# A decode attention block: V products as full-width matmuls, the copy of the products moved behind the next exp, wq loaded first

## The chip, the cores and the metric

The kernel runs on one core of a Trainium2 chip. The metric is the device time of one execution in microseconds: the median of the runs is given for the kernel before. The views of the profile come from one profiled execution on the chip. Its engines are called PE (the matrix engine; PEld is its weight load), DVE (VectorE), ACT (ScalarE), POOL and SP (which issues the loads).

## The reference

One step of decoding for 8 sequences (B = 8, one token each, D = 512). The input is normalised, goes through attention over a cached window and, beside that, through a gated feed-forward network (FFN); the result is x + s * g.

```
xn = layernorm(x)
q  = xn @ wq                        # 32 heads of 128
k, v = the last 1024 positions of the caches, 8 kv heads, each used by 4 q heads
p  = softmax(q @ k.T / sqrt(128))   # per batch and head, over 1024 positions
s  = (p @ v) @ wo
g  = silu((gelu(xn @ w_gate) * (xn @ w_up)) @ w_down)     # F = 1792
out = x + s * g
```

All tensors are bf16. For every batch 2 MB of K and 2 MB of V are read; with the weights that makes 47.46 MB from HBM.

## The kernel before

**Loads.** All large loads go to one ring of eight slots of 16 KB per partition (2 MB each). `load_k` and `load_v` fill a slot with the K or V of one batch in two loads of 1 MB, one for each half of the kv heads (g = 0, 1). SP issues them in the order of the program. Each load waits for its slot to be free and for one of eight semaphores, so the load eight places earlier must have landed. The order is: K 0, wq (two loads of 2 MB), K 1, V 0, and then in iteration b of the loop K b+2 and V b+1. After the loop come gate, up, down and the pieces of wo. The small x goes on ACT's queue.

**Start.** The constants are built on DVE and POOL (L101 to L224: the identity, the mask `neg_st`, `neg_mv`, the selectors `sel`, `own`, `pick`, and a cleared `oT`). The layernorm of x gives `xnR`. DVE turns both halves of K 0 (`turn_k`, L235), and clears `qbd` (L240). The q products (L248) are 32 matmuls of 512 columns into eight PSUM banks; ACT and DVE cast them (L258), DVE turns them (L261), and 16 small copies (L270) place them in `qbd`, a block-diagonal stationary operand.

**Loop over the batches.** Everything is issued in the order of the program on each engine. In iteration b:
- `turn_k(b+1, 0)` turns the first half of the next K on DVE;
- `softmax(b)`: the maximum `mx` on DVE (L306) and its reduction over the four partition groups (L311, L313), `nb` and the exp with its sums on ACT (L316, L318);
- `scores(b+1, 0)`: two mask matmuls (L285) and eight score matmuls of 512 columns (L296) on PE;
- `gather(b-1)`: PE adds the four partition groups of the previous batch's products with `sel` (L361) and the sums (L365), in fp32, into `o_ps`, which holds four batches;
- `turn_k(b+1, 1)` and `scores(b+1, 1)`, the second half;
- `turn_p(b)` turns the probabilities on DVE (L329);
- `values(b)`: the V products (L340), 64 matmuls with 32 stationary and 128 moving columns, which go to four column groups of PE in turn;
- `keep_o(b)`: ACT copies the products from `O_ps` to SBUF (L353). `O_ps` has two buffers.

After batch 4, `regroup(0)` works on the first four batches: the reciprocal of the sums (L376) and a product (L378) on DVE, eight matmuls to `r_ps` on PE (L389), and a cast to `oT` on DVE (L392). On PE these stand behind the V products of batch 4, and on DVE the cast stands ahead of `turn_k(6, 0)`.

**Tail.** `gather(7)`, `regroup(1)`, then the FFN: `z_ps` and `u_ps` (L451), the gelu on ACT and DVE (L461 to L471), a turn (L474), `f_ps` (L480), the gate `g_sb`; then `s_ps`, 128 small matmuls over wo in the order in which its pieces land (L499), `y` (L507), `out_sb` (L509) and the store.

Of the kernel before, what the change touches and what calls it, by code (L numbers as in the profile page):

```python
# [8 lines left out]
ALU = mybir.AluOpType  # L9
AX = mybir.AxisListType  # L10
BF16 = mybir.dt.bfloat16
FP32 = mybir.dt.float32
I32 = mybir.dt.int32
PSUM = bass.MemoryType.PSUM
# [7 lines left out]
def kernel(  # L22
# [13 lines left out]
    nc = tc.nc  # L36

    B, Sq, D = A_x.shape
    Hkv, Sk, Dh = A_k_cache.shape[1], A_k_cache.shape[2], A_k_cache.shape[3]
    Hq = A_wq.shape[1] // Dh  # L40
# [5 lines left out]
    P = nc.NUM_PARTITIONS  # L46
    NK = D // P
    HG = 4
    NG = Hkv // HG
    C = W * HG // P  # L50
# [6 lines left out]
    consts = ctx.enter_context(tc.tile_pool(name="consts", bufs=1))  # L57
    keep = ctx.enter_context(tc.tile_pool(name="keep", bufs=1))
    two = ctx.enter_context(tc.tile_pool(name="two", bufs=2))
    ring = ctx.enter_context(tc.tile_pool(name="ring", bufs=N_SLOTS))  # L60

    def slot(name):
        return ring.tile([P, 2 * ROW], BF16, name=name, tag="slot")
# [6 lines left out]
    def load_cache(cache, b, name):  # L70
        t = slot(name).rearrange("p (g x) -> p g x", g=NG)
        for g in range(NG):
            nc.sync.dma_start(  # L73
                out=t[:, g],
                in_=cache[b, g * HG : (g + 1) * HG, win0:Sk, :].rearrange(
                    "n (p c) d -> p n (c d)", c=C
                ),
            )
        return t

    k_sb, v_sb = {}, {}

    def load_k(b):
        k_sb[b] = load_cache(A_k_cache, b, "k_sb")

    def load_v(b):
        v_sb[b] = load_cache(A_v_cache, b, "v_sb")

    load_k(0)
    wq_v = A_wq.rearrange("(p k) n -> p k n", k=NK)  # L90
    wq_sb = []
    for i in range(2):
        t = slot("wq_sb").rearrange("p (k n) -> p k n", k=NK // 2)
        nc.sync.dma_start(out=t, in_=wq_v[:, i * (NK // 2) : (i + 1) * (NK // 2), :])  # L94
        wq_sb += [t[:, k, :] for k in range(NK // 2)]
    load_k(1)
    load_v(0)


    ident = consts.tile([P, P], BF16, name="ident")  # L100
    nc.vector.memset(ident, 0.0)  # L101
    nc.gpsimd.affine_select(
        out=ident,
        in_=ident,
# [13 lines left out]
        out=xpad,  # L118
        in_=xpad,
# [17 lines left out]
        out=xhat,  # L137
# [9 lines left out]
    with tc.tile_pool(name="ps_x", bufs=1, space=PSUM) as ps_x:  # L147
# [7 lines left out]
        for t in range(4):  # L155
# [4 lines left out]
                start=True,  # L160
                stop=True,
# [5 lines left out]
    qd = Hq // NG  # L167
# [6 lines left out]
        out=hv,  # L174
        in_=hv,
# [7 lines left out]
        out=neg_st,  # L183
        in_=neg_st,
# [8 lines left out]
        out=neg_mv,  # L193
        in_=neg_mv,
# [7 lines left out]


    NU = Hq // 8
    sel = consts.tile([P, NG, Hq], FP32, name="sel")
    nc.vector.memset(sel, 0.0)
    for g in range(NG):
        nc.vector.tensor_reduce(
            out=sel[:, g, g * qd : (g + 1) * qd],
            in_=ident.rearrange("p (t g h) -> p g h t", t=4, g=NG)[:, g],  # L210
            axis=AX.X,
            op=ALU.add,
        )
    own = consts.tile([P, 8], FP32, name="own")
    nc.vector.tensor_reduce(
        out=own, in_=ident.rearrange("p (i e) -> p e i", e=8), axis=AX.X, op=ALU.add
    )
    pick = consts.tile([P, 4 * NU], BF16, name="pick")
    with nc.allow_low_precision(reason="sums of zeros and a single one"):
        nc.vector.tensor_reduce(  # L220
            out=pick, in_=ident.rearrange("p (a e) -> p a e", e=8), axis=AX.X, op=ALU.add
# [7 lines left out]
    qbd = keep.tile([P, 2, B, 2, NG, 4 * Hq], BF16, name="qbd")  # L229
# [3 lines left out]
    def turn_k(b, g):  # L233
        t = kT_pool.tile([P, ROW], BF16, name="kT")
        nc.vector.transpose(out=t.bitcast(I32), in_=k_sb[b][:, g].bitcast(I32))  # L235
        kT[b, g] = t

    turn_k(0, 0)
    turn_k(0, 1)
    nc.vector.memset(qbd, 0.0)  # L240
    q_both = slot("q_both")
    q_bf = q_both[:, 0:ROW]
    q_t = q_both[:, ROW : 2 * ROW]
    with tc.tile_pool(name="ps_q", bufs=1, space=PSUM) as ps_q:
        q_ps = [ps_q.tile([P, 512], FP32, name=f"q_ps{i}") for i in range(8)]
        for k in range(NK):
            for i in range(8):
# [4 lines left out]
                    start=(k == 0),  # L252
                    stop=(k == NK - 1),
# [10 lines left out]
    for j in range(4):  # L264
        sl = slice(32 * j, 32 * j + 32)
        for m in range(2):
            for g in range(NG):
                e = nc.scalar.copy if (4 * j + 2 * m + g) % 3 == 2 else nc.vector.tensor_copy
                c0 = j * Hq + g * qd
                e(out=qbd[sl, m, :, :, g, c0 : c0 + qd], in_=q_v[sl, m, :, 0, :, g, :])  # L270


    pT, S, P_sb, O_ps = {}, {}, {}, {}
    sums = keep.tile([P, B], FP32, name="sums")

    actx = ExitStack()
    ps_s = actx.enter_context(tc.tile_pool(name="ps_s", bufs=2, space=PSUM))
    ps_o = actx.enter_context(tc.tile_pool(name="ps_o", bufs=2, space=PSUM))
    ps_g = actx.enter_context(tc.tile_pool(name="ps_g", bufs=1, space=PSUM))

    def scores(b, g):
# [22 lines left out]
    def softmax(b):  # L304
        mx = two.tile([P, 1], FP32, name="mx")
        nc.vector.tensor_reduce(  # L306
            out=mx, in_=S[b].rearrange("p a c -> p (a c)"), axis=AX.X, op=ALU.max
        )

        m2 = two.tile([64, 1], FP32, name="m2")  # L310
        nc.vector.tensor_tensor(out=m2, in0=mx[0:64, :], in1=mx[64:128, :], op=ALU.max)  # L311
        m1 = two.tile([32, 1], FP32, name="m1")
        nc.vector.tensor_tensor(out=m1, in0=m2[0:32, :], in1=m2[32:64, :], op=ALU.max)  # L313
        nb = two.tile([P, 1], FP32, name="nb")
        for j in range(4):
            nc.scalar.mul(nb[32 * j : 32 * j + 32, :], m1, -inv)  # L316
        P_sb[b] = two.tile([P, C // 2, 32, 2], BF16, name="P_sb")
        nc.scalar.activation(  # L318
            out=P_sb[b].rearrange("p c i w -> p c w i"),
            in_=S[b].rearrange("p a (c w i) -> p (a c) w i", w=2, i=32),  # L320
            func=ACT.Exp,
            bias=nb,
            scale=inv,
            accum_out=sums[:, b : b + 1],
        )

    def turn_p(b):
        pT[b] = two.tile([P, C // 2, Hq, 2], BF16, name="pT")
        nc.vector.transpose(  # L329
            out=pT[b].rearrange("p c h w -> p (c h w)").bitcast(I32),  # L330
            in_=P_sb[b].rearrange("p c i w -> p (c i w)").bitcast(I32),
        )

    def values(b):
        O_ps[b] = ps_o.tile([P, NG, Dh], FP32, name="O_ps")
        for g in range(NG):
            vv = v_sb[b][:, g].rearrange("p (c d) -> p c d", d=Dh)
            for c in range(C):
                t = c % 4
                nc.tensor.matmul(  # L340
                    O_ps[b][32 * t : 32 * t + 32, g, :],
                    pT[b][:, c // 2, :, c % 2],
                    vv[:, c, :],
                    start=(c < 4),
                    stop=(c >= C - 4),
                )

    o_ps = {}
    O_sb = {}

    def keep_o(b):
        O_sb[b] = two.tile([P, NG, Dh], FP32, name="O_sb")
        nc.scalar.copy(out=O_sb[b], in_=O_ps[b])  # L353

    def gather(b):
        q = b % 4
        if q == 0:
            o_ps[b // 4] = ps_g.tile([P, Dh + 1], FP32, name="o_ps")
        o = o_ps[b // 4][32 * q : 32 * q + 32, :]
        for g in range(NG):  # L360
            nc.tensor.matmul(  # L361
                o[:, 0:Dh], sel[:, g, :], O_sb[b][:, g, :], start=(g == 0), stop=(g == NG - 1)
            )
        for g in range(NG):
            nc.tensor.matmul(  # L365
                o[:, Dh : Dh + 1],
                sel[:, g, :],
                sums[:, b : b + 1],
                start=(g == 0),
                stop=(g == NG - 1),  # L370
            )

    def regroup(q):

# [24 lines left out]
    for b in range(B):  # L399
        if b + 2 < B:  # L400
            load_k(b + 2)
        if b + 1 < B:
            load_v(b + 1)
            turn_k(b + 1, 0)
        softmax(b)
        if b + 1 < B:
            scores(b + 1, 0)
        if b >= 1:
            gather(b - 1)
        if b + 1 < B:  # L410
            turn_k(b + 1, 1)
            scores(b + 1, 1)
        turn_p(b)
        values(b)
        keep_o(b)
        if b == 4:
            regroup(0)

# [9 lines left out]
    for u in range(NU):  # L428
        if u % 2 == 0:
            pair = slot("wo_sb").rearrange("p (v j d) -> p v j d", v=2, d=D)  # L430
        t = pair[:, u % 2]
# [5 lines left out]
            nc.sync.dma_start(out=t[:, a:z, :], in_=src[:, a:z, :])  # L437
        wo.append(t)

    gather(B - 1)  # L440
    regroup(1)
    actx.close()
# [4 lines left out]
    for n, ws in (("z_ps", wgu[0]), ("u_ps", wgu[1])):  # L447
        ps = ps_f.tile([P, FT], FP32, name=n)
        for k in range(NK):
            for t in range(4):  # L450
# [4 lines left out]
                    start=(k == 0),  # L455
                    stop=(k == NK - 1),
# [6 lines left out]
        out=z2, in0=z2, scalar1=0.044715, scalar2=1.0, op0=ALU.mult, op1=ALU.add  # L463
# [11 lines left out]
        out=hT.rearrange("p j b -> p (j b)"), in_=h_bf.rearrange("p (y j) -> p j y", j=NJ)  # L475
    )
    f_ps = ps_f.tile([P, DT], FP32, name="f_ps")
    for j in range(NJ):
        for t in range(4):
# [4 lines left out]
                start=(j == 0),  # L484
                stop=(j == NJ - 1),
# [4 lines left out]
        out=g_sb, in0=g_sb, scalar1=0.5, scalar2=0.5, op0=ALU.mult, op1=ALU.add  # L490
# [5 lines left out]
    for u in range(NU):  # L496
        for j in range(8):
            for t in range(4):
# [4 lines left out]
                    start=(u == 0 and j == 0),  # L503
                    stop=(u == NU - 1 and j == 7),
# [7 lines left out]
        out=out_f.rearrange("b (t d) -> t b d", t=4), in_=out_sb[0 : P : RB, :]  # L512
# [31 lines left out]
```

## Time and profile before

| | |
|---|---|
| median of 3 runs | 121.66 us (121.61 to 121.68) |
| the profiled execution | 121.48 us, its span 119.4 us |
| PE busy | 73.0 us (61%), 985 matmul records |
| DVE busy | 75.8 us (63%) |
| ACT busy | 31.4 us (26%) |
| HBM read | 47.46 MB, 397 GB/s over the span |
| main load queue | 94.3% of 16 engines' span |

The span runs from the first to the last instruction of the execution; the execution's own time has 2.1 us around it. The page cuts the span into 40 slices of about 3 us; a digit is the busy share of a slice in tenths, and the row PEclk is the granted clock of PE in tenths of full speed. A line of the timeline gives the start and the duration in us, the engine, the line of the kernel, the operation, the tiles (out<-in), how many instructions are merged, and in brackets the idle time before them and what ended it. Matmul durations include the way through the array, so the distance between starts is what one costs in a row.

### The profile page before, as it was taken

Reading aid. Unit: us, or ns where it says so; the run is one execution under the profiler, and the core shown is the slowest. Engines: PE = TensorE matmul, PEld = TensorE weight load, DVE = VectorE, ACT = ScalarE, POOL = GpSimd, SP = SyncE. Lnnn points to the kernel's source line nnn. Section 1 sums busy time; section 2 is a strip of 40 time slices with the busy share of each in tenths; the row PEclk is TensorE's granted clock in tenths of the full one; section 3 lists DMA queues with packets and bytes.
Section 4 is the critical chain, followed back from the end, with each engine's and each line's share of the span. In section 5 each row is a group of like instructions: output and inputs, shape, how many; then the busy total and the mean of one; then the engine's idle time right before and its main releaser. Section 6 shows DMA issues by size and latency. Waiting matters only on the chain.

```text
span 119.4 us, 2300 instructions
## 1 busy us (share of the span) xinstructions
PE 73.0 (61%) x985; PEld 38.7 (32%) x992; DVE 75.8 (63%) x101; ACT 31.4 (26%) x75; POOL 3.2 (3%) x10
## 2 busy tenths in 40 slices
PE   0001499811994987969687674991994547545370
PEld 0000134300341544535443351450453433143350
DVE  1048978399739999999959959909943241651000
ACT  2233000676007052341712510700616211200000
POOL 2006100000000000000000000000000000000000
PEclk9999999985599999999999998599589855555555
DMA  1999999999999999999999999999999999999930
GB/s 47 411 445 417 434 425 431 417 428 434 428 420 425 431 423 423 428 423 431 417 431 420 431 423 423 428 428 423 420 434 439 437 433 418 427 421 417 412 148 3
DMA packets 6254, 47.61 MB, mean 399 GB/s; under 512 B 732, under 2 KB 868, under 8 KB 1124
## 3 DMA queue, kind: packets, MB, share of 16 engines
q1 hardware_dynamic: 6228, 47.46, 94.3%
q8 instruction: 8, 0.13, 0.4%
q10 hardware_dynamic: 16, 0.01, 0.0%
q14 instruction: 2, 0.02, 0.0%
HBM read 47.46 MB, written 0.01 MB: 397 GB/s over the span
## 4 chain that ended last, share of the span: by engine, by line
DMA 85%; DVE 6%; PE 4%; SPq 2%; issue 1%
DMA k_sb<-in_A_k_cache_dram 48%; DMA wo_sb<-in_A_wo_dram 20%; DMA v_sb<-in_A_v_cache_dram 17%; DVE kT L235 4%; PE S_ps L296 2%; PE s_ps L499 1%; SPq L73 1%; DVE mx L306 1%; SPq L94 1%; PE O_ps L340 1%; PE r_ps L389 1%; DVE y L507 0%; DVE out_sb L509 0%; DVE oT L392 0%; DVE m L311 0%
## 5 line engine op out<-in xcount | busy, mean ns | idle before, releaser
L296 PE MATMUL S_ps<-kT,qbd 128*128 128x512 bf16 x128 | 34.1, 413 | 15.5 <-DVE kT L235 11.9
L235 DVE STREAM_TRANSPOSE kT<-k_sb 128x2048 int32<-128x2048 int32 x16 | 36.5, 2289 | 4.4 <-DMA k_sb<-in_A_k_cache_dram 4.3
L296 PEld LDWEIGHTS <-qbd 128*128 128x128 bf16 x128 | 12.8, 102 | 31.9 <-issue 16.4
L248 PE MATMUL q_ps<-wq_sb,xnR 128*128 128x512 bf16 x32 | 9.8, 481 | 4.3 <-DMA wq_sb<-in_A_wq_dram 4.3
L316 ACT ACTIVATE nb<-m 32x1 f32<-32x1 f32 x32 | 6.4, 201 | 22.5 <-DVE m L313 22.2
L306 DVE TENSOR_REDUCE mx<-S_ps 128x1 f32<-128x1024 f32 x8 | 9.6, 1196 | 4.1 <-PE S_ps L296 4.1
L318 ACT ACTIVATE P_sb<-S_ps,nb 128x1024 bf16<-128x1024 f32 x8 | 11.1, 1390 | 0.3
L340 PE MATMUL O_ps<-v_sb,pT 128*32 128x128 bf16 x512 | 9.1, 226 | 2.6 <-DVE pT L329 2.6
L340 PEld LDWEIGHTS <-pT 128*32 128x32 bf16 x512 | 7.6, 100 | 5.6 <-issue 3.0
L353 ACT COPY O_sb<-O_ps 128x256 f32<-128x256 f32 x8 | 3.0, 372 | 23.3 <-PE O_ps L340 23.3
L329 DVE STREAM_TRANSPOSE pT<-P_sb 128x512 int32<-128x512 int32 x8 | 5.7, 711 | 3.4 <-ACT P_sb L318 3.3
L248 PEld LDWEIGHTS <-xnR 128*128 128x128 bf16 x32 | 3.7, 118 | 10.1 <-issue 8.1
L361 PE MATMUL o_ps<-O_sb,sel 128*32 128x128 f32 x32 | 6.3, 332 | 0.9 <-ACT O_sb L353 0.9
L499 PE MATMUL s_ps<-wo_sb,oT 128*32 128x128 bf16 x128 | 4.4, 307 | 3.7 <-DMA wo_sb<-in_A_wo_dram 3.7
L258 ACT CAST q_both<-q_ps 128x512 bf16<-128x512 f32 x6 | 3.0, 611 | 12.2 <-PE q_ps L248 12.2
L151 PE MATMUL xnT_ps<-ident,xhat 8*128 8x8 bf16 x4 | 0.3, 174 | 8.9 <-DVE xhat L136 8.9
L499 PEld LDWEIGHTS <-oT 128*32 128x32 bf16 x128 | 3.5, 136 | 4.7 <-issue 4.5
L361 PEld LDWEIGHTS o_ps<-O_sb,sel 128*32 128x32 f32 x32 | 3.4, 128 | 5.0 <-issue 1.7
L507 DVE TENSOR_TENSOR y<-s_ps,g_sb 128x128 f32<-128x128 f32 x1 | 0.3, 292 | 7.2 <-PE s_ps L499 7.2
L285 PE MATMUL S_ps<-neg_mv,neg_st 128*128 128x512 bf16 x9 | 3.3, 384 | 1.9 <-DVE q_both L258 1.9
L129 DVE BATCH_NORM_STATS2 stats<-x_sb 8x6 f32<-8x512 bf16 x1 | 0.7, 681 | 5.7 <-DMA x_sb<-in_A_x_dram 5.7
L240 DVE MEMSET qbd<- 128x4096 uint32 x1 | 3.5, 3472 | 0.8 <-issue 0.8
(64 smaller groups left out, 51.2 us busy)
## 6 DMA issues: line engine op xcount, KB each, us to landing
k_sb<-in_A_k_cache_dram SPq DMA_DIRECT2D x16, 1024.0 KB, 19.7
v_sb<-in_A_v_cache_dram SPq DMA_DIRECT2D x16, 1024.0 KB, 20.0
wq_sb<-in_A_wq_dram SPq DMA_DIRECT2D x2, 2048.0 KB, 11.4
wo_sb<-in_A_wo_dram SPq DMA_DIRECT2D x3, 1024.0 KB, 25.1
wgu_sb<-in_B_w_gate_dram SPq DMA_DIRECT2D x1, 1792.0 KB, 21.4
wgu_sb<-in_B_w_up_dram SPq DMA_DIRECT2D x1, 1792.0 KB
wd_sb<-in_B_w_down_dram SPq DMA_DIRECT2D x1, 1792.0 KB
wo_sb<-in_A_wo_dram SPq DMA_DIRECT2D x1, 640.0 KB
```

Source lines behind the costliest of these rows:

```text
L235: nc.vector.transpose(out=t.bitcast(I32), in_=k_sb[b][:, g].bitcast(I32))
L240: nc.vector.memset(qbd, 0.0)
L248: nc.tensor.matmul(q_ps[i], xnR[:, k, :, :].rearrange("p j b -> p (j b)"), wq_sb[k][:, i * 512 : (i + 1) * 512], start=(k == 0), stop=(k = ...
L285: nc.tensor.matmul(S[b][:, half, :], neg_st.rearrange("p j h -> p (j h)"), neg_mv.rearrange("p a n -> p (a n)"), start=True, stop=False,)
L296: nc.tensor.matmul(S[b][:, half, :], qbd[:, m, b, w, g, :], kv[:, half * 16 : (half + 1) * 16, m, :, w], start=False, stop=(g == NG - 1 an ...
L306: nc.vector.tensor_reduce(out=mx, in_=S[b].rearrange("p a c -> p (a c)"), axis=AX.X, op=ALU.max)
L316: nc.scalar.mul(nb[32 * j : 32 * j + 32, :], m1, -inv)
L318: nc.scalar.activation(out=P_sb[b].rearrange("p c i w -> p c w i"), in_=S[b].rearrange("p a (c w i) -> p (a c) w i", w=2, i=32), func=ACT.Exp,
L329: nc.vector.transpose(out=pT[b].rearrange("p c h w -> p (c h w)").bitcast(I32), in_=P_sb[b].rearrange("p c i w -> p (c i w)").bitcast(I32),)
L340: nc.tensor.matmul(O_ps[b][32 * t : 32 * t + 32, g, :], pT[b][:, c // 2, :, c % 2], vv[:, c, :], start=(c < 4), stop=(c >= C - 4),)
L361: nc.tensor.matmul(o[:, 0:Dh], sel[:, g, :], O_sb[b][:, g, :], start=(g == 0), stop=(g == NG - 1))
L499: nc.tensor.matmul(s_ps[32 * t : 32 * t + 32, :], oT[:, j, u, :], wo[u][:, j, t * DT : (t + 1) * DT], start=(u == 0 and j == 0), stop=(u = ...
```

## The change

- **V products.** `values` now takes four of the 32 chunks of positions at a time: a stationary operand of 128 columns (four chunks x 32 heads) and 512 moving columns (four chunks x 128), 16 matmuls per batch instead of 64. Of the 4 x 4 blocks of each result only the four on the diagonal are wanted. `O_ps` is four times as wide, two PSUM banks, and has one buffer instead of two.
- **Copy and gather.** `keep_o` copies the upper and the lower 64 partitions with the two blocks that each needs; `sel` has one more dimension to pick the diagonal; the gather has four products instead of two, and one product for the sums instead of two, with a selector `sel_s` of its own.
- **Order on ACT.** The copy of batch b-1's products is issued after the exp of batch b, not at the end of iteration b-1.
- **Start.** wq is loaded ahead of K of batch 0; on DVE `qbd` is cleared before K 0 is turned, and the second half of K 0 is turned after the copies to `qbd`.
- **Addresses.** An unused tile `pad` of 128 bytes per partition is allocated; with it the ring starts on a multiple of 512 bytes, as it did.

```diff
-    load_k(0)
     wq_v = A_wq.rearrange("(p k) n -> p k n", k=NK)
...
+    load_k(0)
     load_k(1)
     load_v(0)
...
-    sel = consts.tile([P, NG, Hq], FP32, name="sel")
+    sel = consts.tile([P, NG, 2, Hq], FP32, name="sel")
...
+    consts.tile([P, 32], FP32, name="pad")
+    sel_s = consts.tile([P, Hq], FP32, name="sel_s")
...
+    nc.vector.memset(qbd, 0.0)
     turn_k(0, 0)
-    turn_k(0, 1)
-    nc.vector.memset(qbd, 0.0)
...
+    turn_k(0, 1)
...
-    ps_o = actx.enter_context(tc.tile_pool(name="ps_o", bufs=2, space=PSUM))
+    ps_o = actx.enter_context(tc.tile_pool(name="ps_o", bufs=1, space=PSUM))
...
-        O_ps[b] = ps_o.tile([P, NG, Dh], FP32, name="O_ps")
+        O_ps[b] = ps_o.tile([P, NG, 4 * Dh], FP32, name="O_ps")
         for g in range(NG):
-            vv = v_sb[b][:, g].rearrange("p (c d) -> p c d", d=Dh)
-            for c in range(C):
-                t = c % 4
+            vv = v_sb[b][:, g]
+            for c in range(0, C, 4):
                 nc.tensor.matmul(
-                    O_ps[b][32 * t : 32 * t + 32, g, :],
-                    pT[b][:, c // 2, :, c % 2],
-                    vv[:, c, :],
-                    start=(c < 4),
-                    stop=(c >= C - 4),
+                    O_ps[b][:, g, :],
+                    pT[b][:, c // 2 : c // 2 + 2].rearrange("p c h w -> p (c h w)"),
+                    vv[:, c * Dh : (c + 4) * Dh],
+                    start=(c == 0),
+                    stop=(c == C - 4),
                 )
...
-        O_sb[b] = two.tile([P, NG, Dh], FP32, name="O_sb")
-        nc.scalar.copy(out=O_sb[b], in_=O_ps[b])
+        O_sb[b] = two.tile([P, NG, 2, Dh], FP32, name="O_sb")
+        for a in range(2):
+            rows = slice(64 * a, 64 * a + 64)
+            nc.scalar.copy(
+                out=O_sb[b][rows].rearrange("p g w d -> p g (w d)"),
+                in_=O_ps[b][rows, :, 2 * a * Dh : 2 * (a + 1) * Dh],
+            )
...
-            nc.tensor.matmul(
-                o[:, 0:Dh], sel[:, g, :], O_sb[b][:, g, :], start=(g == 0), stop=(g == NG - 1)
-            )
-        for g in range(NG):
-            nc.tensor.matmul(
-                o[:, Dh : Dh + 1],
-                sel[:, g, :],
-                sums[:, b : b + 1],
-                start=(g == 0),
-                stop=(g == NG - 1),
-            )
+            for w in range(2):
+                nc.tensor.matmul(
+                    o[:, 0:Dh],
+                    sel[:, g, w, :],
+                    O_sb[b][:, g, w, :],
+                    start=(g == 0 and w == 0),
+                    stop=(g == NG - 1 and w == 1),
+                )
+        nc.tensor.matmul(
+            o[:, Dh : Dh + 1], sel_s, sums[:, b : b + 1], start=True, stop=True
+        )
...
         softmax(b)
+        if b >= 1:
+            keep_o(b - 1)
...
         values(b)
-        keep_o(b)
...
+    keep_o(B - 1)
     gather(B - 1)
```

More of the change, by code (lines that the diff above doesn't have):

```diff
@@ L208 @@
         nc.vector.tensor_reduce(
-            out=sel[:, g, g * qd : (g + 1) * qd],
-            in_=ident.rearrange("p (t g h) -> p g h t", t=4, g=NG)[:, g],
+            out=sel[:, g, :, g * qd : (g + 1) * qd],
+            in_=ident.rearrange("p (a g h w) -> p g w h a", a=2, g=NG, w=2)[:, g],
             axis=AX.X,
@@ L213 @@
         )
+    consts.tile([P, 32], FP32, name="pad")
+    sel_s = consts.tile([P, Hq], FP32, name="sel_s")
+    nc.vector.tensor_reduce(
+        out=sel_s, in_=ident.rearrange("p (j h) -> p h j", j=4), axis=AX.X, op=ALU.add
+    )
     own = consts.tile([P, 8], FP32, name="own")
@@ L360, in gather @@
         for g in range(NG):
-            nc.tensor.matmul(
-                o[:, 0:Dh], sel[:, g, :], O_sb[b][:, g, :], start=(g == 0), stop=(g == NG - 1)
-            )
-        for g in range(NG):
-            nc.tensor.matmul(
-                o[:, Dh : Dh + 1],
-                sel[:, g, :],
-                sums[:, b : b + 1],
-                start=(g == 0),
-                stop=(g == NG - 1),
-            )
+            for w in range(2):
[8 more added lines that the diff above has]
+            o[:, Dh : Dh + 1], sel_s, sums[:, b : b + 1], start=True, stop=True
+        )
     def regroup(q):
```

## The prediction

> **What bounds the kernel now.** I read the slices of the page first, then its chain, then the timeline of one middle batch, of the place where batch 4 ends, and of the tail. M(b) below is the start of `mx` (L306) in batch b.
>
> The slices: clock, DMA and rate.
>
> ```profile
> PEclk9999999985599999999999998599589855555555
> DMA  1999999999999999999999999999999999999930
> GB/s 47 411 445 417 434 425 431 417 428 434 428 420 425 431 423 423 428 423 431 417 431 420 431 423 423 428 428 423 420 434 439 437 433 418 427 421 417 412 148 3
> ```
>
> The DMA row is full from slice 2 on: 47.46 MB go through at about 425 GB/s without a hole, and the last weights land at 114.8. The chain agrees:
>
> ```profile
> DMA 85%; DVE 6%; PE 4%; SPq 2%; issue 1%
> ```
>
> So compute counts only where it makes the end wait, or makes the queue run dry. Slot waits do not make it dry: a cache load takes about 20 us from issue to landing (section 6 of the page), so some 8 MB are queued ahead. The question is how late compute may be. One batch of the timeline, columns start, us, engine, line:
>
> ```profile
> 48.34 1.19 DVE L306 TENSOR_REDUCE mx<-S_ps 128x1 f32<-128x1024 f32 x1
> 50.52 0.62 PE L361 MATMUL o_ps<-O_sb,sel 128*32 128x128 f32 x4
> 50.80 1.39 ACT L318 ACTIVATE P_sb<-S_ps,nb 128x1024 bf16<-128x1024 f32 x1
> 52.17 1.90 PE L296 MATMUL S_ps<-kT,qbd 128*128 128x512 bf16 x8 [0.93 <-DVE kT L235]
> 54.00 1.08 PE L340 MATMUL O_ps<-v_sb,pT 128*32 128x128 bf16 x64
> 55.10 1.19 DVE L306 TENSOR_REDUCE mx<-S_ps 128x1 f32<-128x1024 f32 x1
> ```
>
> The period is 6.76 us, and VectorE is full in it (1.19 + 0.3 + 2.29 + 0.71 + 2.27); PE has gaps. A batch of cache takes the queue 9.85 us (K of batch 5 lands at 61.08, of batch 6 at 70.9), so from batch 4 on M(b) is set by K: 63.3, 73.2, 83.05. The end of batch 4, and the tail:
>
> ```profile
> 69.99 0.66 PE L389 MATMUL r_ps<-pick,o_x 128*128 128x16 bf16 x8
> 70.68 0.43 DVE L392 CAST oT<-r_ps 128x128 bf16<-128x128 f32 x1 [1.35 <-PE r_ps L389]
> 70.92 2.32 DVE L235 STREAM_TRANSPOSE kT<-k_sb 128x2048 int32<-128x2048 int32 x1
> ...
> 89.18 1.23 DVE L306 TENSOR_REDUCE mx<-S_ps 128x1 f32<-128x1024 f32 x1 [1.49 <-PE S_ps L296]
> 98.70 0.67 PE L389 MATMUL r_ps<-pick,o_x 128*128 128x16 bf16 x8 [1.58 <-DVE o_x L378]
> 106.28 1.69 PE L480 MATMUL f_ps<-wd_sb,hT 128*32 128x128 bf16 x56 [2.90 <-DVE hT L474]
> 108.38 1.04 PE L499 MATMUL s_ps<-wo_sb,oT 128*32 128x128 bf16 x32 [0.41 <-DMA wo_sb<-in_A_wo_dram]
> 114.84 1.25 PE L499 MATMUL s_ps<-wo_sb,oT 128*32 128x128 bf16 x32 [0.49 <-DMA wo_sb<-in_A_wo_dram]
> 116.15 0.29 DVE L507 TENSOR_TENSOR y<-s_ps,g_sb 128x128 f32<-128x128 f32 x1 [7.20 <-PE s_ps L499]
> ```
>
> Two things are to be seen. VectorE, which works in order, cannot turn the next K (70.92) before the `oT` cast, and that waits for `r_ps`, which PE issues behind the V products of batch 4; today this ends just as K lands. And after `r_ps` of the tail the FFN runs and then waits for wo. Slack of the tail: f_ps and s_ps need 1.36 (106.28 to the next weight load at 107.64) + 4 x 0.87 (1.04 less the end of the last matmul) = 4.85 us of PE at the half clock seen there, so f_ps could start at 116.15 - 0.3 - 4.85 = 111.0, and `r_ps`, 7.6 earlier, at 103.4. **The slack is 4.7 us** over 98.70.
>
> **The change, part by part**, against the profiled execution: 121.48 us, span 119.4, 2.1 around it. The median of the runs is 0.18 above it.
>
> *V products.* Out: 64 matmuls, 1.08 us. In: 16 of 512 columns on a 128-column weight. The scores have that shape: 18 in a row took 3.81 us in the q products (from 19.21: 0.212 each); at a granted clock of 0.50 the scores of batch 0 started every 0.43 us (29.36, 29.78, 30.21). So 3.4 us, or 6.8 cold, per batch: +2.3, or more. [...]
>
> *Gather.* From L361 to L365 four fp32 passes took 0.46 (43.76 to 44.22), the four for the sums 0.19. Now eight and two: 1.02 instead of 0.65.
>
> *Copy of the products.* One of 128x256 took 0.37; now two of 64x512. The casts of 128x512 took 0.61 alone, six of them 3.03, so 0.48 apart: the pair 0.48 + 0.61 = 1.1. It now follows the next batch's exp, which ends at M + 3.94 (34.78 to 38.72). Nothing but the gather waits for it, and the next V products, since `O_ps` has one buffer; in the loop they come later anyway.
>
> *Start.* wq takes K's place: its halves land by about 8.8 and at 13.6 (where K 0 and the first half of wq land today: the first q matmul waits until 13.71), K of batch 0 at about 16.0 and 18.4. The q products start when `xnR` is there, about 9.95 instead of 13.71, and end at 18.5 to 20.2 instead of 23.0, according to when they go from 0.43 to 0.21 us each (today after 5.5 us). The qbd copies follow as now, 6.4 later. The qbd memset (3.5 us) and the extra constants (0.5) end at 15.8, under K's landing. K 0's second half is turned after the copies, at the cost of nothing: PE takes 1.7 to 3.4 us for the first half's scores. M(0) comes at 30 to 31 instead of 34.8. SP issues the same loads, in the same order from K 1 on; K 2's second half waits until 13.6 for its semaphore, with over 10 MB queued. No byte is saved, so the stream ends at 114.8 as before.
>
> *Loop.* End of scores to end of scores on PE: 3.4 + 10 x 0.212 + 1.02 + 8 x 0.212 = 8.3 us. PE, not VectorE, sets the period now. M(1) = 37.5, M(2) about 45.6, M(3) 53.9, then 62.2, but K 5 lands at 61.08 and its turn takes 2.3: M(4) = 63.4, as today. The 4 us won at the start are given back here.
>
> *End of batch 4.* Exp ends 67.3, copy 68.4, gather 69.5, second scores 71.2, V products 74.6, `r_ps` 75.2, cast 75.7, K 6 turned 78.0. M(5) = 78.0 instead of 73.16, **4.8 us later**: the cover, K's landing, is gone.
>
> *To the end*, at full clock. M(5) + 3.94 + 1.1 + 1.05 + 1.7 + 0.25 = 86.1 = M(6). M(7) = 86.1 + 8.2 = 94.3 (89.18 today). Then exp 98.2, copy of batch 6 99.35, gather 100.4, V 103.8, copy 105.2, gather 106.3, reciprocal and product (1.6) 107.9 = `r_ps`. That is 9.2 late, 4.5 over the slack. f_ps at 107.9 + 7.6 = 115.5, s_ps through at 120.35, y at 120.7, **4.5 us behind 116.15**.
>
> *Clock.* With the FFN and s_ps at full clock (V products run 17 ns a matmul there, s_ps 27) y would come at 117.8: +1.6. The other way, PE idles from 75.8 to 78.0 for the cast; today gaps of 2.3 us (71.0 to 73.29) and 2.55 us (80.6 to 83.18) were followed by half clock for about 3.4 us. If such a stretch falls on a gather and second scores, it costs 0.85 + 1.7 = 2.5, on V products up to 3.4 more. I take neither end: FFN at half, batches 5 to 7 mostly full. [...]
>
> *Ring padding.* `sel` grows by 256 bytes, pad and `sel_s` add 128 each, two `O_sb` buffers 1024 each: 2560 = 5 x 512. The ring moves by whole 512-byte blocks, so I cost it at nothing; the trace has no second placement. Bounds from the slices: 412 to 445 GB/s around 425, so -5 to +3% of the stream; I take zero because packets stay as they are, and a faster stream could not pull in an end that compute sets.
>
> *Slots.* The load of wo's third megabyte waits for V of batch 5 (89.3 instead of 80.3); it is issued at about 88 today. One us late with 25 us from issue to landing (section 6): nothing runs dry.
>
> **The rivals.** (a) *The tail stays under wo*: `r_ps` by 103.4, time as before, 121.7. It needs V products at some 1 us each or batch 4's cast not behind them; the order of PE and VectorE speaks against it. 5%. (b) *The stream speeds up*, the one mechanism for faster: if ring placement or the 770 fewer PE instructions took 1% off the stream, wo lands 1.1 us earlier, 120.6. It decides only if (a) holds too. Against: 512-byte blocks before and after, and instruction queues of 0.4% of the DMA time. 4%. (c) *Clock full to the end*: 121.66 + 1.6 = 123.3 up to 124.5. 18%. (d) *Cold in the long products of batches 5 to 7*: +6.5 to +8, 128.2 to 129.7. 15%. My forecast, 58%: 121.66 + 4.5 = 126.2.
>
> **The numbers.** About 0.2% is what a measurement of this kernel can tell from no change. Faster 0.04, same 0.05, slower 0.91. The range leaves out (a), (b) and the far end of (d): 123.0 to 129.0.
>
> **What would show it.** Right: L344's 16 matmuls at 3.4 us or more; M(0) near 30.5, M(4) near 63.4, M(5) near 78; the `oT` cast near 75.5; s_ps in one run with no wait for wo; the chain ending in PE, ACT and VectorE, no longer in DMA. Wrong: M(5) near 73, a wait of s_ps for wo, or DMA slices with holes before 100 us.

## The result, and the profile after

The changed kernel takes **128.18 us** (median of 6 runs, 127.10 to 128.76), the kernel before 121.63 us in the same comparison: the ratio is 1.0537, 95% interval 1.0511 to 1.0563. It is 6.55 us slower. The profiled execution took 128.54 us with a span of 126.5. Ratios, here and below, leave out runs more than 1.5% above the fastest of their kernel; medians hold all runs.

The page of the changed kernel, first the three slice rows, then the line of the chain by engine:

```profile
PEclk9999999855999999999999999995999999985559
DMA  4999999999999999999999999999999999990000
GB/s 104 446 426 399 432 425 425 435 422 422 435 422 425 427 427 419 438 425 422 432 427 412 435 432 414 438 430 417 447 434 430 418 420 423 435 371 30 5 5 3
...
PE 57%; DVE 19%; ACT 12%; DMA 5%; issue 3%; ACTq 1%; DVEq 0%
```

A slice is now 3.16 us. The stream runs as full as before and is through in slice 36, at about 114 us; the last four slices are empty. The chain, 85% DMA before, is 57% PE and holds 5% DMA, all of it the load of x at the start. So nothing was lost in the stream; the end has moved from it to compute.

Two batches of the timeline of the changed kernel (start, us, engine, line):

```profile
47.47 3.61 PE L344 MATMUL O_ps<-v_sb,pT 128*128 128x512 bf16 x16
47.67 1.23 DVE L311 TENSOR_REDUCE mx<-S_ps 128x1 f32<-128x1024 f32 x1 [1.15 <-PE S_ps L301]
51.52 1.16 ACT L359 COPY O_sb<-O_ps 64x512 f32<-64x512 f32 x2
53.18 1.06 PE L371 MATMUL o_ps<-O_sb,sel 128*32 128x128 f32 x8
54.21 1.91 PE L301 MATMUL S_ps<-kT,qbd 128*128 128x512 bf16 x8
56.16 1.23 DVE L311 TENSOR_REDUCE mx<-S_ps 128x1 f32<-128x1024 f32 x1 [1.60 <-PE S_ps L301]
...
76.38 0.61 PE L398 MATMUL r_ps<-pick,o_x 128*128 128x16 bf16 x8
77.03 0.43 DVE L401 CAST oT<-r_ps 128x128 bf16<-128x128 f32 x1 [4.25 <-PE r_ps L398]
77.27 2.31 DVE L240 STREAM_TRANSPOSE kT<-k_sb 128x2048 int32<-128x2048 int32 x1
79.51 1.18 DVE L311 TENSOR_REDUCE mx<-S_ps 128x1 f32<-128x1024 f32 x1
84.52 1.06 PE L371 MATMUL o_ps<-O_sb,sel 128*32 128x128 f32 x8 [2.99 <-ACT O_sb L359]
85.55 3.50 PE L301 MATMUL S_ps<-kT,qbd 128*128 128x512 bf16 x8
89.09 1.23 DVE L311 TENSOR_REDUCE mx<-S_ps 128x1 f32<-128x1024 f32 x1 [2.75 <-PE S_ps L301]
97.66 1.23 DVE L311 TENSOR_REDUCE mx<-S_ps 128x1 f32<-128x1024 f32 x1 [3.88 <-PE S_ps L301]
111.30 0.66 PE L398 MATMUL r_ps<-pick,o_x 128*128 128x16 bf16 x8 [1.58 <-DVE o_x L387]
119.59 3.63 PE L510 MATMUL s_ps<-wo_sb,oT 128*32 128x128 bf16 x128
123.27 0.29 DVE L518 TENSOR_TENSOR y<-s_ps,g_sb 128x128 f32<-128x128 f32 x1 [2.48 <-PE s_ps L510]
```

The period from `mx` to `mx` is 8.49 us instead of 6.76, and the bracket says who sets it: DVE, full before, now waits 1.6 us for PE. At the end of batch 4 DVE sits idle 4.25 us ahead of the cast, because `r_ps` is behind the long V products; `mx` of batch 5 comes at 79.5 instead of 73.2. In batch 5 PE waits 2.99 us for the copy of the products, and the eight scores behind it take 3.50 us instead of 1.91: the granted clock was at half from about 85.7 to 89.1. In the tail all 128 matmuls of `s_ps` run in one piece, with no wait for wo.

### The profile page after: what moved, and what is told of

The parts are those of the page before. It is cut to its first block, busy times and chain, and to the rows that moved or that the text cites. A ratio compares the mean times of both kernels' runs of the same rounds, so it can differ in the third digit from the quotient of the medians.

```text
span 126.5 us, 1590 instructions
## 1 busy us (share of the span) xinstructions
PE 90.9 (72%) x624; PEld 45.3 (36%) x624; DVE 76.5 (60%) x102; ACT 36.9 (29%) x83; POOL 3.2 (3%) x10
## 4 chain that ended last, share of the span: by engine, by line
PE 57%; DVE 19%; ACT 12%; DMA 5%; issue 3%; ACTq 1%; DVEq 0%
PE S_ps L301 20%; PE O_ps L344 17%; PE q_ps L252 7%; PE o_ps L371 6%; DMA x_sb<-in_A_x_dram 5%; ACT P_sb L323 5%; DVE mx L311 4%; ACT O_sb L359 3%; DVE kT L240 3%; PE s_ps L510 3%; DVE qbd L274 2%; ACT nb L321 2%; PE S_ps L290 1%; PE f_ps L491 1%; DVE q_both L265 1%
## 5 line engine op out<-in xcount | busy, mean ns | idle before, releaser
L301 PE MATMUL S_ps<-kT,qbd 128*128 128x512 bf16 x128 | 33.6, 409 | 7.4 <-DVE kT L240 3.9
L344 PE MATMUL O_ps<-v_sb,pT 128*128 128x512 bf16 x128 | 29.0, 380 | 0.0
L344 PEld LDWEIGHTS <-pT 128*128 128x128 bf16 x128 | 12.5, 98 | 15.3 <-issue 0.8
L371 PE MATMUL o_ps<-O_sb,sel 128*32 128x128 f32 x64 | 8.5, 276 | 6.3 <-ACT O_sb L359 6.3
L359 ACT COPY O_sb<-O_ps 64x512 f32<-64x512 f32 x16 | 9.2, 575 | 4.8 <-PE O_ps L344 4.7
L371 PEld LDWEIGHTS o_ps<-O_sb,sel 128*32 128x32 f32 x64 | 6.3, 109 | 10.0 <-ACT O_sb L359 8.3
L290 PE MATMUL S_ps<-neg_mv,neg_st 128*128 128x512 bf16 x16 | 4.8, 378 | 1.9 <-DVE q_both L262 1.9
L491 PE MATMUL f_ps<-wd_sb,hT 128*32 128x128 bf16 x56 | 1.7, 312 | 4.1 <-DVE hT L485 4.1
```

The lines of the kernel that those rows point to most:

```text
L290: nc.tensor.matmul(S[b][:, half, :], neg_st.rearrange("p j h -> p (j h)"), neg_mv.rearrange("p a n -> p (a n)"), start=True, stop=False,)
L301: nc.tensor.matmul(S[b][:, half, :], qbd[:, m, b, w, g, :], kv[:, half * 16 : (half + 1) * 16, m, :, w], start=False, stop=(g == NG - 1 an ...
L344: nc.tensor.matmul(O_ps[b][:, g, :], pT[b][:, c // 2 : c // 2 + 2].rearrange("p c h w -> p (c h w)"), vv[:, c * Dh : (c + 4) * Dh], start= ...
L359: nc.scalar.copy(out=O_sb[b][rows].rearrange("p g w d -> p g (w d)"), in_=O_ps[b][rows, :, 2 * a * Dh : 2 * (a + 1) * Dh],)
L371: nc.tensor.matmul(o[:, 0:Dh], sel[:, g, w, :], O_sb[b][:, g, w, :], start=(g == 0 and w == 0), stop=(g == NG - 1 and w == 1),)
```

## The experiments

Ratios are to the kernel before, run beside each; in brackets the 95% interval. M(b) is the start of `mx` in batch b, the last column that of `y`, both from the one profiled run of each kernel. Edits are shown shortened.

| kernel | us | ratio | M(0) | M(4) | M(5) | M(6) | M(7) | y |
|---|---|---|---|---|---|---|---|---|
| before | 121.6 | 1 | 34.8 | 63.3 | 73.2 | 83.1 | 89.2 | 116.2 |
| changed | 128.18 | 1.0537 | 32.9 | 64.6 | 79.5 | 89.1 | 97.7 | 123.3 |
| start alone | 121.23 | 0.9973 | 32.5 | 63.1 | 73.1 | 82.9 | 88.6 | 115.9 |
| cast late | 122.66 | 1.0088 | 32.0 | 63.8 | 74.1 | 82.8 | 90.7 | 116.6 |
| copy first | 126.87 | 1.0354 | 32.7 | 65.3 | 78.9 | 85.6 | 93.9 | 121.0 |
| half of V | 126.79 | 1.0437 | 32.9 | 65.4 | 78.1 | 87.7 | 95.7 | 120.9 |
| masks as filling | 127.44 | 1.0477 | 31.8 | 63.6 | 78.5 | 88.1 | 96.6 | 122.1 |
| x first | 125.46 | 1.0322 | 30.9 | 63.4 | 77.8 | 85.8 | 94.3 | 119.9 |
| both moves | 122.52 | 1.0090 | 32.4 | 65.0 | 74.8 | 82.8 | 89.6 | 116.9 |
| both moves, shifted | 121.50 | 0.9997 | 32.3 | 64.9 | 74.8 | 82.9 | 89.5 | 116.3 |

The eight kernels here that have the new start with x on ACT's queue differ in M(0) by up to 1.0 us (31.8 to 32.9), though their programs are the same up to there or nearly so. A later M that is up to 1 us earlier is therefore no finding by itself; the distances from M to M are.

My theory: wide V products make PE the bound of the loop, and the cast behind them in batch 4 turns that into a loss that the tail cannot take up. Rival 1: the new start costs it. Rival 2: PE is the bound everywhere, the cast is only beside it. Rival 3: the copy behind the exp, with one `O_ps` buffer, costs it.

**The start alone.**

```diff
-    load_k(0)                 # ahead of wq, in the kernel before
+    load_k(0)                 # behind wq
-    turn_k(0, 0); turn_k(0, 1); memset(qbd)
+    memset(qbd); turn_k(0, 0)     # and turn_k(0, 1) behind the qbd copies
```

> The kernel before with only the new start: wq ahead of K 0, qbd cleared first, the second half of K 0 turned after the qbd copies; narrow V products, old gather and copy. Theory (the wide V products and the cast behind them are the loss): the loop stays at 6.8 us a batch, batch 4 onward is set by K, the end by wo: 121.6, within 0.3 us of the kernel before; mx of batch 0 near 32.5, mx of batch 5 near 73. Rival 1 (the new start is the loss: x lands at 8.74 instead of 7.02 behind wq): 124 or more.

Measured: 121.23 us, ratio 0.9973 (0.9962 to 0.9984). Rival 1 falls. The late x shows (8.63 instead of 7.02), but is far from the end. The part is a small gain, 0.3 us, which I had not expected: the last piece of wo is used from 114.58 instead of 114.84, and the first slice carries 89 GB/s instead of 47. SP issues the two wq loads, 4 MB, in 0.87 us, where it took 1.30 for the 2 MB of K 0. That the earlier stream is the gain is read from these rows and not tested by itself.

**The old start with everything else changed.**

```diff
-    load_k(0)                 # behind wq, in the changed kernel
+    load_k(0)                 # ahead of wq; the DVE order as before
```

> The changed kernel with the old start (K 0 ahead of wq, both halves of K 0 turned ahead of the qbd memset); all else as changed. Theory: mx of batch 0 back at 34.8, and since PE sets the loop at 8.5 us a batch from there, mx of batch 4 comes at 66.6 instead of 64.6 and all that follows 1.9 later: 130.1 (129 to 131, by where the clock falls). Rival 1 (the start is the loss): 123 or less.

Measured: 129.06 us, ratio 1.0596 (1.0567 to 1.0626). M(4) is 66.8 (expected 66.6), 2.1 behind the changed kernel, and from M(0) on, at 35.0, the two are alike: 31.8 us to M(4) in both. The loss is in the other parts.

**The cast moved.**

```diff
         turn_k(b + 1, 1)
         scores(b + 1, 1)
+        if b == 5: cast_o(0)     # the cast of regroup(0), taken out of it
         turn_p(b)
```

> The changed kernel with one instruction of VectorE moved: the cast of the first four batches to oT stands in iteration 5 ahead of the turn of the probabilities, not at the end of iteration 4 ahead of the turn of K 6. Theory: K 6 is turned at 72.8, right behind the product for r_ps, and mx of batch 5 starts near 75.1 instead of 79.5; PE has no gap there, so no half clock on the second scores of batch 6 (1.1 to 1.7 us): 122.7 (122 to 124.5). Rival 2 (PE is the bound throughout, and the cast is only beside it): no change, 127.5 to 128.5.

Measured: 122.66 us, ratio 1.0088 (1.0064 to 1.0111). On DVE the next `mx` no longer waits:

```profile
74.05 1.18 DVE L311 TENSOR_REDUCE mx<-S_ps 128x1 f32<-128x1024 f32 x1
77.76 0.39 DVE L406 CAST oT<-r_ps 128x128 bf16<-128x128 f32 x1
```

From M(4) to M(5) it takes 10.3 us instead of 14.9 (M(4) itself is 0.9 earlier, as M(0) is), and M(6), at 82.75, is set by the landing of K again. PE waits 0.77 us ahead of the gather instead of 2.99, and the granted clock stays full until about 105. 5.5 of the 6.55 us are back, with the V products as wide as ever. Rival 2 falls. The place of one cast of 0.4 us, with what follows from it, was five sixths of the loss. `r_ps` of the tail comes at 104.38, 1.0 us behind the 103.4 up to which the tail has slack.

**The copy ahead of the exp again.**

```diff
-        if b >= 1:
-            keep_o(b - 1)        # behind softmax(b)
         ...
         values(b)
+        keep_o(b)
```

> The changed kernel with the copy of the products back at the end of its own iteration, ahead of the next batch's exp on ACT. Theory: the exp of the next batch now waits for the V products and the copy, ends about 7.4 instead of 5.3 us after the scores; in the loop PE's own 8.5 us still set the period, but the last batch has nothing behind which to hide it: V of batch 7 starts 2 us later, 130.2. Rival 3 (the single O_ps buffer and the copy behind the exp are the loss): faster than the changed kernel, 126 or less.

Measured: 126.87 us, ratio 1.0354 (1.0288 to 1.0420), which is 125.9 us; the four runs spread from 125.00 to 127.41, and the profiled one took 127.03. I had forecast a loss of 2 us, and by the ratios it gained about 2. Batch 5 of its timeline:

```profile
75.94 1.17 ACT L359 COPY O_sb<-O_ps 64x512 f32<-64x512 f32 x2 [4.98 <-PE O_ps L344]
79.00 3.22 PE L301 MATMUL S_ps<-kT,qbd 128*128 128x512 bf16 x8 [2.41 <-DVE kT L240]
82.15 1.36 PE L371 MATMUL o_ps<-O_sb,sel 128*32 128x128 f32 x8
83.48 1.91 PE L301 MATMUL S_ps<-kT,qbd 128*128 128x512 bf16 x8
```

The copy of batch 4 is done at 77.1, while PE and DVE wait for the cast, so the gather needs no exp and the scores follow at once: M(6) comes 6.8 us after M(5) instead of 9.6. Not all of these 2.8 us are the wait: here the slow scores are the first half, right behind the gap of the cast (79.00, 3.22 us instead of 1.91). By the run with x first below, which has the copy behind the exp and its slow scores at that same place, and takes 7.99 us, 1.6 us are the place of the slow stretch and 1.2 the wait. The loss in the tail is there too (from M(7) to the reciprocal 13.8 us instead of 12.1), 1.7 us. So the new place of the copy is good in the last batch and bad where the batch begins late; rival 3 holds for about 2 of the 6.55 us, by the wait of the gather, with the clock, and not by the single buffer, which the V products of the changed kernel never waited for.

**Half of the V products.**

```diff
-            for c in range(0, C, 4):
+            for c in range(0, C // 2, 4):
```

> The changed kernel with 8 of the 16 V products per batch (it leaves out the second half of the positions of each head group). Theory A (the V products on PE are the loop's period): 1.73 us less on PE per batch, period 6.8, the end back under wo: 121.7. Theory B, which the run with the copy ahead of the exp suggests (the copy behind the exp is a second chain, nearly as long: exp end at mx + 3.94, copy 1.22, gather 1.08, second scores 1.75, 0.2 = 8.2 us from mx to mx): the period only falls from 8.5 to 8.2, mx of batch 4 near 64.3, of batch 5 near 77.5, of batch 7 near 94, 122.8.

Measured: 126.79 us, ratio 1.0437 (1.0407 to 1.0467). The period is 8.04 us (M(2) 49.29, M(3) 57.33, M(4) 65.36), not 6.8. PE now has time and waits, in every batch:

```profile
54.35 1.06 PE L371 MATMUL o_ps<-O_sb,sel 128*32 128x128 f32 x8 [1.20 <-ACT O_sb L359]
57.33 1.22 DVE L311 TENSOR_REDUCE mx<-S_ps 128x1 f32<-128x1024 f32 x1 [1.15 <-PE S_ps L301]
```

That is theory B: behind the V products there is a second chain, exp, copy, gather, second scores, only 0.45 us shorter. Half of the new work on PE, taken out, buys that much a batch. Its time is above the 122.8 that B gave, at least in part because the granted clock was down in three places of the loop: from M(1) to M(2) it took 9.6 us, with the second scores at 45.81 taking 3.45 us instead of 1.91; from M(5) to M(6) 9.6 us, with a granted clock of 0.5 in the slice from 83.8 to 86.9; and the slice from 99.3 to 102.4 shows 0.6.

**Masks as filling.**

```diff
-            for half in range(2):              # mask matmuls
+            for i in range(12 if b == 6 else 2):
```

> The changed kernel with the two mask matmuls of batch 6 issued six times over (ten more matmuls of 512 columns, about 2.15 us, in the time in which PE waits for the turn of K 6 behind the cast). Theory: PE's idle stretch of 2.2 us at 77.3 is what the clock answers with half speed on the second scores of batch 6; filled, these take 1.9 instead of 3.5 and mx of batch 6 comes 8.5 instead of 9.6 us after that of batch 5: 126.5 to 127. Rival (the clock falls for another reason): no change, 127.5 to 128.5.

Measured: 127.44 us, ratio 1.0477 (1.0447 to 1.0508); M(0) is 1.0 us earlier, which masks of batch 6 cannot cause, and from there to `y` it takes 90.3 us, where the changed kernel takes 90.4. In batch 5 nothing was gained: M(6) still comes 9.6 behind M(5). A miss:

```profile
75.81 2.75 PE L291 MATMUL S_ps<-neg_mv,neg_st 128*128 128x512 bf16 x12
83.48 1.27 PE L372 MATMUL o_ps<-O_sb,sel 128*32 128x128 f32 x8 [2.98 <-ACT O_sb L360]
84.74 3.30 PE L302 MATMUL S_ps<-kT,qbd 128*128 128x512 bf16 x8
```

The gap behind the cast is filled, and the scores are slow all the same. The second gap, the gather's 2.98 us wait for the copy, is still there, and in the 3.41 us before the clock fell at about 84.2, as long as the slow stretch that followed, PE was at work for 0.7 us.

**x first.**

```diff
-    for r in range(0, B, 2):
-        nc.scalar.dma_start(out=x_sb[r : r + 2], ...)
+    nc.sync.dma_start(out=x_sb, ...)       # ahead of wq
```

> The changed kernel with x loaded in one piece by SP ahead of wq, not by ACT beside it. Theory: x lands near 3 instead of 8.7, the q products start when the first half of wq lands (about 9.2 instead of 11.7), mx of batch 0 near 30.4 instead of 32.9; PE's period carries this to batch 4, where K stops it at 63.4 (now 64.64): 1.25 us earlier, 126.9. If the start is worth nothing, 128.2.

Measured: 125.46 us, ratio 1.0322 (1.0303 to 1.0341): twice the expected gain. M(4) is at 63.39, stopped by K as expected (1.25 us). Most of the rest is the clock:

```profile
77.91 3.45 PE L300 MATMUL S_ps<-kT,qbd 128*128 128x512 bf16 x8 [2.20 <-DVE kT L239]
82.79 1.06 PE L370 MATMUL o_ps<-O_sb,sel 128*32 128x128 f32 x8 [1.43 <-ACT O_sb L358]
```

Here it fell in the gap behind the cast, at about 77.7, the slow scores filled time in which the gather waits anyhow, and M(6) follows M(5) in 7.99 us instead of 9.58.

**The ring's place**, in the kernel before: 128 unused bytes per partition, and 256.

```diff
+    consts.tile([P, 32], FP32, name="pad")      # ring_off128
+    consts.tile([P, 64], FP32, name="pad")      # ring_off256
```

> The kernel before with an unused tile of 128 bytes per partition, so that the ring starts 128 bytes off a multiple of 512 (and of 256). [...] If place does not matter: 121.6.

> The kernel before with 256 unused bytes per partition, so that the ring starts on a multiple of 256 but not of 512. [...]

Measured: at 128 bytes 122.81 us, ratio 1.0096 (1.0081 to 1.0112); at 256 bytes 121.45 us, 0.9997 (0.9983 to 1.0010), where a ring that needs a multiple of 512 would have shown about 122.8 again. At 128 the last piece of wo is used from 116.25 instead of 114.84. So place matters here: 128 bytes off cost 1%, 256 bytes off nothing. The padding of the change keeps a multiple of 256, so by these runs it should neither win nor lose; the changed kernel was not run without it.

**Both moves.** The cast late, and the copy behind the exp only where it helps:

```diff
         softmax(b)
-        if b >= 1:
+        if b == B - 1:
             keep_o(b - 1)
         ...
         values(b)
+        if b < B - 2:
+            keep_o(b)
```

> The changed kernel, still with wide V products, with two moves: the cast to oT of the first four batches in iteration 5 (as in the run with the late cast), and the copy of the products at the end of its own iteration for batches 0 to 5, behind the next exp only for batch 6. Theory (the loss is the cast that stands ahead of K 6, and a gather that waits for exp and copy in the batches where PE has time to wait; the V products themselves cost 8.5 us a batch, which is less than the 9.85 of the stream): mx of batch 5 near 75.5, of batch 6 near 83, of batch 7 near 90, y near 116, so the tail is back under wo: 121.3 to 121.9. Rival (wide V products cannot be hidden at all): 122.5 or more, as with the late cast alone.

> The same, with x loaded by SP ahead of wq. Theory: compute has 1 us more in hand, the end is set by the stream, which starts some 0.3 us later for the load of x: 121.3 to 121.9, no faster than without.

Measured: 122.52 us, ratio 1.0090 (1.0062 to 1.0119); with x first 122.26 us, 1.0099 (1.0062 to 1.0136), the same within the intervals. Neither is faster than the late cast alone (1.0088), though `r_ps` now comes at 103.19, within the slack. All M(b) came as expected, but y at 116.85 did not. The tail of the first:

```profile
114.60 0.48 PE L520 MATMUL s_ps<-wo_sb,oT 128*32 128x128 bf16 x9 [0.35 <-DMA wo_sb<-in_A_wo_dram]
115.98 0.83 PE L520 MATMUL s_ps<-wo_sb,oT 128*32 128x128 bf16 x23 [0.90 <-issue]
```

wo is there at 114.60, much as in the kernel before. Nine matmuls later PE stands still for 0.90 us and waits for nothing that the profile shows. One packet of the instruction queue, 0.02 MB, moved between 112 and about 115.2, behind which nothing moves up to 117.5. The late cast alone, with the same program on PE, begins these 128 matmuls at 113.42 and runs them in one row of 3.09 us; the changed kernel shows no stop there either. Nor is the stop the whole loss: the median span is 120.0 us against 119.45 for the kernel before, and another 0.5 us lies outside the span (2.57 us instead of 2.07), where the traces show nothing.

**The same, shifted**: 112 tiny matmuls, 224 instructions, ahead of batch 0's masks.

```diff
         if g == 0:
             S[b] = ps_s.tile([P, 2, 512], FP32, name="S_ps")
+            for i in range(112 if b == 0 else 0):
+                nc.tensor.matmul(S[b][0:32, 0, 0:16], neg_st[:, 0, :], neg_mv_flat[:, 0:16], start=True, stop=True)
```

> The kernel with wide V products and both moves (wide_mended), with 112 tiny matmuls (32 stationary, 16 moving columns, on the mask operands, into scores that are overwritten) ahead of the first mask matmuls of batch 0, where PE waits 3.9 us for qbd. Its question is the 0.9 us for which PE stood still inside s_ps after wo had landed, with one packet of 0.02 MB on the instruction queue in that stretch. Theory (PE waits for its next instructions at a fixed place of its program): 224 instructions more ahead of it move the place out of s_ps into PE's idle time before f_ps; y comes near 116.0 and the time is 121.5 to 121.9, level with the kernel before. Rival (the stop belongs to the matmuls or to the landing of wo): y stays at 116.8, 122.4.

Measured: 121.50 us, ratio 0.9997 (0.9985 to 1.0009). The kernel with wide V products is level with the one before. The median span is 119.5 us, 0.5 less than without the 112 matmuls, and the time outside it is back at 2.10; what moved that second half microsecond is open.

```profile
114.59 1.01 PE L528 MATMUL s_ps<-wo_sb,oT 128*32 128x128 bf16 x25 [0.38 <-DMA wo_sb<-in_A_wo_dram]
115.91 0.29 PE L528 MATMUL s_ps<-wo_sb,oT 128*32 128x128 bf16 x7 [0.31 <-issue]
```

The stop has moved and shrunk to 0.31 us, so it belongs to a place of the program and not to these matmuls. It did not go where I sent it: it is 16 matmuls later, not 112 earlier. 16 matmuls are 32 instructions; why 224 more ahead of the stop move it by 32 is not shown. It ends at nearly the same time in the three traces whose rows show it (115.98 with both moves, 116.22 with x first as well, 115.91 here), so the later place waited less. What PE waits for until then is open; that it is its next instructions is not shown.

The fastest of all is the start alone, 121.23 us: the one part of the change that helps, with the narrow V products.

## Why the prediction was right, and what it missed

- **What bounds.** Right: the stream did not move, compute became the end, and the slack of 4.7 us was overrun.
- **V products.** Right: the 16 take 3.45 us a batch (47.63 to 51.08 in the chain), against the 3.4 worked out from the rows of the q products (0.212 each).
- **Loop.** Right, 8.49 instead of 8.3 (the terms as written add up to 8.24). But the prediction gave the period to PE alone. Half the V products gave back only 0.45 us of it: exp, copy and gather are a second chain nearly as long.
- **Batch 4.** Right in mechanism and nearly in size: M(5) 79.5 against 78.0, and moving the cast brought back 5.5 us. Of the 1.5 us between the two, 1.25 were there in M(4).
- **Copy.** Right that the V products come later anyway, too short where it had nothing else but the gather wait for the copy. After the late batch 5 the gather waits 2.99 us for it, and the scores behind the gather wait with it; the sum for M(6) held that chain, the sentence on the copy did not. Its undoing is worth 1.8%, 2 us, with what it moved of the clock. That gain and the cast's do not add up: with the cast late, the other place of the copy brought nothing more that the intervals show.
- **Start.** Mis-sized. x was taken to land as before; it landed at 8.74 instead of 7.02, beside two loads of 2 MB, and the q products started at 11.67, not 9.95. M(0) came at 32.9, not 30.5, and M(4) 1.25 us late, which x first took back.
- **Clock.** The price of the slow stretch was right in kind (scores 1.6 us longer), but it was left out of the likeliest case. The prediction had it follow the gap behind the cast; in the profiled run it followed the gather's wait, and filling the first gap changed nothing. With x first and with the copy first it did follow the first gap. What decides which one it is, the runs do not show (last section), so for this term a right number would have been luck.
- **The sum.** 128.18 against 126.2. Up to M(7) compute ran 3.4 us later than forecast: start 1.25, clock 1.6, and 0.5 more, in part the copy (1.22 with its start, not 1.1) and the period. The FFN gave 0.8 back (f_ps 6.8 us behind `r_ps`, not 7.6), with z and part of u at full clock. `y` is 2.6 us behind the sum in the profiled run, the median 2.0.
- **Rivals.** (a), that the tail stays under wo, did not come about in this kernel, but it does once the cast and the copy are moved (`r_ps` at 103.19): wide V products can be hidden, and with the stop moved the time is level. The measured 128.18 stands at the lower edge of (d), but not by its mechanism: the V products of batches 5 to 7 took 3.61 to 3.74 us each, from the first start to the last end, not 6.8.
- **Padding.** Costed at nothing. The run at 256 bytes agrees, in the kernel before; the bound for it was sound, since a ring at 128 bytes cost 1%.

## What to carry to other kernels

When a stream sets the end, ask of every longer operation not what it adds but what stands behind it in order on another engine: here 2.4 us of PE per batch were free, and one short cast placed behind them on the engine that turns the next K was not. An order that helps in the last batch can hurt in one that starts late, so a copy's place is worked out for each of the two. And a change of several parts is worth taking apart: its start alone was faster than either kernel.

## What the runs showed of the hardware

- **Instructions.** With both moves PE stopped for 0.90 us in a row of small matmuls, with nothing to wait for that the profile shows. With 224 more instructions ahead of it the stop came 32 instructions later and took 0.31 us, and the median span was 119.5 us instead of 120.0, 0.4% less. The cause is not shown.
- **Placement.** The loads are mostly of 8 KB and more per partition. Into a ring 128 bytes off a multiple of 256 the kernel before took 122.81 us against 121.59 (ratio 1.0096); into one 256 bytes off a multiple of 512 it took 121.45 against 121.52 (0.9997). What makes the first slower is not shown.
- **Clock.** In the kernel before, the granted clock falls to half at 26.1, 73.9, 84.1 and 94.4 and is full again at 32.9, 77.3 and 87.5: all of these are multiples of 3.41 us apart. At 84.1 PE had been at work for 0.9 of the 3.41 us before. In the changed kernel it falls at 85.7 and 113.0 and rises at 89.1, and with x first it falls at 77.7 and rises at 81.1: the same step from other origins. In the changed kernel the 3.41 us up to 78.85 and up to 82.27 had PE at work for 2.0 and 1.9 us and the clock stayed full, and the 3.41 us up to 85.7, with 1.2 us, ended in the fall; with x first the 3.41 us up to 77.7 did so with 1.4. In the changed kernel 1.7 us up to 37.9 kept the clock and 1.8 up to 113.0 lost it, so no sharp limit is shown. Nor did the fall come at once: the 3.41 us up to 84.5 had PE at work for 0.4 us, and the clock stayed full for 1.2 us more. In these runs a mostly idle stretch was enough, and where the slow one began decided whether it fell on work that counts; what sets that moment is not shown.
- **Small loads.** Four loads of 2 KB for x, issued by ACT in the first 2.4 us, landed at 7.02 beside K 0 (the kernel before) and at 8.74 beside wq (the changed kernel); one load of 8 KB ahead of wq on SP (x first) landed at 2.4.
